# Heads of the last unit but one turned behind their own block, short cycles moved from tile 65 to tile 75, last projection pair stored behind its cycle's block

## The chip, the core and the metric

The kernel runs on one core of a Trainium2 chip. A core has five engines that run side by side, each in its own order: TensorE (PE, matmuls; PEld is its weight load), VectorE (DVE), ScalarE (ACT), GpSimd (POOL) and SyncE (SP, which issues the transfers between the core's memory and the chip's main memory). The metric is the device time of one execution in microseconds (us), as the median of several runs.

## The reference

A layer norm of x (2048 tokens of 512 numbers), then two branches on it, joined by a gate:

```python
xn = _layernorm(x, axis=-1)
# s: attention with 32 heads of 16, softmax over all 2048 keys
q, k, v = (xn @ wqkv) split into 3 x 32 heads x 16
p = softmax(q k^T * 16**-0.5)
s = (p v) @ wo
# g: gated unit with 1792 inner columns, no nonlinearity inside, silu at its end
g = silu(((xn @ w_gate) * (xn @ w_up)) @ w_down)
return x + s * g
```

All inputs and outputs are float32.

## The kernel before

**Units, tiles, cycles.** Attention is cut into 32 units: unit i is a group of 4 heads (8 groups) with 512 queries (4 column chunks). A unit has 16 key tiles of 128 keys, so tiles count from 0 to 511, and tile n belongs to unit n // 16. For each tile and head TensorE computes the transposed scores ("t", L755), ACT their exps into a tile e (L757), and TensorE multiplies the exps by the values ("pv", L774; "last" for unit 31). Ahead of that, by 86 matmuls, run the untransposed scores ("s", L733), of which DVE takes the maxima (L735); a unit's maxima go through main memory into two extra rows of the queries.

The work is put out in cycles of BLOCK = 5 tiles. SHORT gives some cycles another length. A cycle holds 20 t, 20 s (none after the scores have run out, near tile 491) and a filler pair; then `values` puts out, in this order: the list `before_values`, the maxima of a finished unit, one step of `heads`, the block (the pv matmuls of the cycle's tiles, and the sum), the list `behind_values`, and up to four bulk transfers. The last cycle has two tiles and ends with the block of unit 31's last tiles.

**The block** (`part_block`) multiplies into one bank per unit, and then adds it: the first block of a unit is copied by ACT (L782), later ones are copied by ACT to the one tile `part` (L787) and added by POOL (L788, shown at L100, the helper that records POOL's and SP's instructions), and from tile 492 on DVE adds straight from the bank (L784). When a unit's tile 15 is in, `finish(i)` turns and scales its heads: transpose (L799), reciprocal (L803), product (L805), transpose back (L810) and a store to OD (L811); then unit i is in `finished`. `finish` is a generator: for units before 28 it yields once, for units 28 and 29 twice, for unit 30 never. It is put on a list and stepped later: `heads` one step per cycle ahead of the block, `last_group` (units 28 and 29) at three places within a cycle's items.

**The filler** is a generator of pairs of matmul groups, one for the lower 64 rows of the array and one for the upper 64; `Filler.item` puts out one matmul of a half, and fetches the next pair as soon as one is used up. If the generator yields nothing, there is no pair until the start of the next cycle, and that cycle has no filler if there is none then either. LIMIT caps the items per half that a cycle takes. In order the filler gives:

- 13 projection pairs of keys and queries (`proj_pair`). At a pair's end ACT copies one half to `qr`, DVE the other (`rest`, on `before_values`), and `store` (on `behind_values`) lets POOL split both into a high and a low part in `hl`, of which there is one buffer, and stores each to KD or QD.
- 80 pairs of the gated unit (`ffn`): g and u pairs (product on DVE, L449; ACT's copy of g, L494) and y pairs. Its pool is opened where the projection's pool is closed, and takes over its memory.
- the output projection (`ending`): z pairs for chunk 3 (all but its last rows), then z0, z1 and z2, two of four token tiles each (`two_tiles(c, t)`), each of which waits in `until(c)` for the split rows of chunk c. `prepare` reloads the rows of a chunk from OD when its units are in `finished` (the last fourth of chunk 2 needs unit 30), and POOL splits them (`o_split`) six steps later; `end` multiplies a tile by its gate (L581), and the sum with x (L590) and the store follow behind the block.

Each cycle's items are ordered by a written list in ORDERS where there is one for its counts, and evenly otherwise. DVE, ACT, POOL and TensorE keep the order of the program; the issues of SP are ordered by the scheduler. In the last stage there are five banks for the transposed scores. The end of the program (`last_heads`, L815 on, and four pairs of matmuls at L683) turns the heads of unit 31 and finishes the last four token tiles.

Of the kernel before, what the change touches and what calls it, by code (L numbers as in the profile page):

```python
# [22 lines left out]
NC = S // 512  # L23
# [43 lines left out]
}  # L67
SHORT = {65: 3, 68: 3}
LIMIT = {65: 12, 491: 12}
BULK = 4  # L70
EBUFS = 20
HBUFS = 1
# [13 lines left out]
def body(ctx, tc, x, wqkv, wo, wg, wu, wd, out):  # L86
# [23 lines left out]
    def dma(dst, src):  # L110
        sync.dma_start(dst, src)
# [42 lines left out]
    def psum(tag, name):  # L154
        ps, bufs = fst["ps"]
        return ps.tile([P, 512], F32, tag=tag, name=name, bufs=bufs[tag])
# [11 lines left out]
    def flush():  # L168
        while waiting:
            waiting.pop(0)[1]()  # L170
# [6 lines left out]
    before_values, behind_values, lighter = [], [], [False]  # L177

    def run_all(queue):
        while queue:  # L180
            queue.pop(0)()
# [6 lines left out]
    def part_tile():  # L188

        return ep.tile([P, 512], F32, name="part", bufs=1)  # L190
# [84 lines left out]
    def late():  # L275
        return now[0] > NU * NT - LEAD // 4
# [82 lines left out]
    def qk_weights(m, which):  # L359
        c0 = which * D + m * P  # L360
        return split(f"w{which}", wqkv[:, c0:c0 + P])
# [21 lines left out]
    def proj_pair(m, which):  # L383

        two = Pair([("misc", f"p{w}_{m}_{c}") for _, w, c in which],
                   [terms(lambda d: ws[0][:, d], lambda d: ws[1][:, d],
                          lambda d: xh[c][:, d], lambda d: xl[c][:, d], ND) for ws, _, c in which])
        yield two
        outs = two.outs
        raws = [qp.tile([P, D], F32, name="qr", bufs=QBUFS) for _ in outs]  # L390
        fst["high"] = nc.scalar.activation(raws[0], outs[0], AF.Copy)

        def rest():
            nc.vector.tensor_copy(raws[1], outs[1])
            behind_values.append(lambda: store(raws))

        def store(raws):
            for o, (_, w, c) in zip(raws, which):
                hl = qp.tile([P, 2, D], F32R, name="hl", bufs=HBUFS)
                split_rows(o, hl[:, 0], hl[:, 1])  # L400
                qk_store(hl, m, w, c)
        before_values.append(rest)
# [59 lines left out]
    def gu_weights(f):  # L462
        fs = slice(f * P, (f + 1) * P)
        return [split(n, w[:, fs]) for n, w in (("w1", wg), ("w0", wu))]
# [223 lines left out]
    NU = NG * NC  # L688
# [71 lines left out]
    def block(todo):  # L760

        for i in sorted({i for i, _, _ in todo}):
            part_block(i, [t for t in todo if t[0] == i])

    def part_block(i, todo):

        g = i // NC
        whole = i == NU - 1
        o = fst["last"] if whole else psum("b", f"pv{i}")
        for n, (_, kt, es) in enumerate(todo):  # L770
            halves = [slice(0, 256), slice(256, 512)] if whole and kt == NT - 1 else [slice(0, 512)]
            for c, j in ((c, j) for c in halves for j in range(4)):
                h0 = (4 * g + j) * VW
                nc.tensor.matmul(o[32 * j:32 * j + 32, c], V[:, kt, h0:h0 + 32], es[j][:, c],  # L774
                                 start=(kt if whole else n) == 0, stop=kt == NT - 1 if whole else n == len(todo) - 1,
                                 skip_group_check=whole)
        if whole:
            if todo[-1][1] == NT - 1:
                last_heads(o)
        elif todo[0][1] == 0:  # L780
            sums[i] = keep.tile([P, 512], F32, name="acc", bufs=2)
            nc.scalar.activation(sums[i], o, AF.Copy)  # L782
        elif late():
            nc.vector.tensor_tensor(sums[i], o, sums[i], op=OP.add)  # L784
        else:
            part = part_tile()
            nc.scalar.activation(part, o, AF.Copy)  # L787
            pool.tensor_tensor(sums[i], sums[i], part, op=OP.add)  # L788
        if not whole and todo[-1][1] == NT - 1:
            (last_group if NU - NC <= i < NU - 2 else heads).append(finish(i))  # L790

    def finish(i):

        g, c = divmod(i, NC)
        tr = keep.tile([P, 16, 32], F32, name="tr", bufs=1)
        acc = sums.pop(i)
        late = i >= NU - NC
        flat = "p b e -> p (b e)"
        nc.vector.transpose(tr.rearrange(flat), acc)  # L799
        rc = keep.tile([P, 16, 1], F32, name="rc", bufs=1)  # L800
        if NU - NC <= i < NU - 2:
            yield
        nc.vector.reciprocal(rc, tr[:, :, DH:DH + 1])  # L803
        over = rc.to_broadcast([P, 16, DH])
        (nc.vector if i >= NU - NC else pool).tensor_tensor(tr[:, :, 0:DH], tr[:, :, 0:DH], over, op=OP.mult)  # L805
        if not late:
            yield
        elif i < NU - 2:
            yield
        nc.vector.transpose(acc, tr.rearrange(flat))  # L810
        dma(OD[c][4 * g:4 * g + 4], acc)  # L811
        finished.add(i)


    def last_heads(o):  # L815

        tr = keep.tile([P, 16, 32], F32, name="tr", bufs=1)
        rc = keep.tile([P, 16, 1], F32, name="rc", bufs=1)
        both, fst["t"] = [fst["fp"].tile([P, 512], F32, name="g", bufs=2).bitcast(F32R) for _ in range(2)]
        back = keep.tile([P, 512], F32, name="acc", bufs=2)  # L820
        both = both.rearrange("p (b e) -> p b e", e=32)
        flat = "p b e -> p (b e)"
        for h in range(2):
            c, b = slice(256 * h, 256 * h + 256), slice(8 * h, 8 * h + 8)
            nc.vector.transpose(tr[:, b].rearrange(flat), o[:, c])
            nc.vector.reciprocal(rc[:, b], tr[:, b, DH:DH + 1])
            nc.vector.tensor_tensor(tr[:, b, 0:DH], tr[:, b, 0:DH], rc[:, b].to_broadcast([P, 8, DH]), op=OP.mult)
            pool.tensor_copy(both[:, b, 0:DH], tr[:, b, 0:DH])
            pool.tensor_tensor(both[:, b, DH:32], tr[:, b, 0:DH], both[:, b, 0:DH], op=OP.subtract)
        for h in range(2):  # L830
            c, b = slice(256 * h, 256 * h + 256), slice(8 * h, 8 * h + 8)
            nc.vector.transpose(back[:, c], both[:, b].rearrange(flat).bitcast(F32))
            nc.scalar.activation(fst["t"][:, c], back[:, c], AF.Copy)


    def run(gen):
        for _ in gen:
            pass
# [124 lines left out]
    def filler(wq0):  # L963
        yield from proj_pair(0, [(wq0, 0, 2), (wq0, 0, 3)])
        for m in range(1, NG // 2):
            wk, wq = fst["qk", m]
            for c in range(NC):
                if c == 2 and m + 1 < NG // 2:
                    fst["qk", m + 1] = qk_weights(m + 1, 1), qk_weights(m + 1, 0)
                yield from proj_pair(m, [(wk, 1, c), (wq, 0, c)])  # L970
                if m == 1 and c:
                    bulk.extend(lambda n=n, src=src[c], c=c, d=d: dma(XD[c][n][:, d].bitcast(F32), src[:, d].bitcast(F32))
                                for n, src in enumerate((xh, xl)) for d in range(ND))
                if m == NG // 2 - 1 and c == NC - 2:
                    nxt = gu_weights(0)
        run_all(before_values)
        run_all(behind_values)
        run_all(bulk)
        flush()
        qkv.close()  # L980
        fst["fp"] = ffp.enter_context(tc.tile_pool(name="ffn", bufs=1, reuse_waits="tile"))
        yield from ffn(nxt)
# [3 lines left out]
    heads, last_group = [], []  # L986
# [92 lines left out]
    with tc.manual_schedule(engines=ORDERED):  # L1079
        with banks_of(EARLY_BUFS):  # L1080
            fil = Filler(filler(early()))
        place_of = banks_of(BUFS)
        q, m, n = 0, LEAD, 0
        while n < NU * NT:
            tiles = min(SHORT.get(n, BLOCK), NU * NT - 2 - n) or 2
            ends = n + tiles == NU * NT
# [4 lines left out]
            if fil.done:  # L1091
                fil = Filler(ending())
            f = fil.begin(LIMIT.get(n, 99))
            last = min(4 * (n + tiles), TOTAL - 4 * (not ends))
# [51 lines left out]
```

## Time and profile before

| | us |
|---|---|
| median of 3 runs (lowest, highest) | 1686.39 (1685.56, 1687.9) |
| the profiled execution, its time | 1685.45 |
| its span, first to last instruction | 1683.7 |
| PE busy | 1667.0 (99%) |
| DVE busy | 1418.4 (84%) |
| ACT busy | 1188.1 (71%) |
| POOL busy | 736.6 (44%) |

The mean granted clock of TensorE is 0.995 of full speed. Matmuls are pipelined, so a busy PE in the table is not PE at its peak. In the profile's rows a group of instructions is "line engine operation out<-in xcount"; in a timeline the start and the length stand ahead of it, and idle time of the engine before it, with what ended it, in brackets behind it. In a table of stretches each row has the bounds, the length, the busy time of the five engines with counts, the granted clock, the DMA engines' share and GB/s.

### The profile page before, as it was taken

How to read it: one execution, taken by the hardware profiler on the slowest of the kernel's cores; microseconds unless marked ns; L12 is line 12 of the kernel's file. 1: busy time of each engine (PE TensorE's matmuls, PEld its weight loads, DVE VectorE, ACT ScalarE, POOL GpSimd, SP SyncE). 2: the span in 40 equal slices, each digit the busy share in tenths (PEclk: the TensorE clock that was granted, in tenths of full speed). 3: DMA queues.
4: the chain of work that ended last, by engine and by line, in shares of the span. 5: the costliest groups of instructions: out<-in, count | busy, mean ns of one | idle time of the engine just before them, and what ended most of it. 6: DMA issues, size and time to landing. Idle time of an engine off the chain costs nothing.

```text
span 1683.7 us, 35313 instructions
## 1 busy us (share of the span) xinstructions
PE 1667.0 (99%) x13702; PEld 1123.8 (67%) x13702; DVE 1418.4 (84%) x2477; ACT 1188.1 (71%) x2553; POOL 736.6 (44%) x772
## 2 busy tenths in 40 slices
PE   9999999999999999999999999999999999999997
PEld 6776666666666676666667666766676676666654
DVE  7888888888888998798889888888988898899822
ACT  6367777776766787677677767867787677678673
POOL 5214434651634456155252733624365262455551
PEclk9999999999999999999999999999999999999998
DMA  7434335321321313121142212302233121133241
GB/s 272 139 123 173 134 120 160 104 66 36 86 55 55 105 53 96 43 74 55 37 103 91 72 50 64 101 18 64 80 99 91 36 74 36 46 104 98 71 129 51
DMA packets 124467, 145.94 MB, mean 87 GB/s; under 512 B 13644, under 2 KB 75340, under 8 KB 123532
## 3 DMA queue, kind: packets, MB, share of 16 engines
q1 hardware_dynamic: 124300, 143.69, 27.7%
q8 instruction: 108, 1.77, 0.4%
q14 instruction: 59, 0.48, 0.1%
HBM read 95.94 MB, written 47.45 MB: 85 GB/s over the span
## 4 chain that ended last, share of the span: by engine, by line
PE 96%; DVE 2%; ACT 0%; DMA 0%; POOL 0%; issue 0%; SPq 0%; DVEq 0%; POOLq 0%; ACTq 0%
PE pv L774 26%; PE s L733 16%; PE t L755 14%; PE g L355 10%; PE u L355 9%; PE y L355 9%; PE p L355 4%; PE z L355 2%; DVE mx L735 2%; PE last L774 1%; PE v L307 1%; PE v L327 1%; PE p L307 1%; PE warm L865 0%; DMA KD<-hl 0%; PE xT L283 0%
## 5 line engine op out<-in xcount | busy, mean ns | idle before, releaser
L735 DVE TENSOR_REDUCE mx<-s 128x1 f32<-128x512 f32 x2048 | 1244.9, 682 | 192.7 <-PE t L755 134.3
L757 ACT ACTIVATE e<-t 128x512 f32<-128x512 f32 x2048 | 1024.4, 669 | 23.9 <-PE t L755 20.3
L755 PE MATMUL t<-qs,ks 50*128 50x512 f32 x2048 | 789.9, 406 | 1.9 <-DVE mx L735 1.4
L733 PE MATMUL s<-ks,qs 48*128 48x512 f32 x2048 | 757.4, 407 | 1.5 <-ACT part L787 1.4
L733 PEld LDWEIGHTS s<-ks,qs 48*128 48x128 f32 x2048 | 367.7, 186 | 140.3 <-issue 83.1
L774 PE MATMUL pv<-e,V 128*32 128x512 f32 x3968 | 446.5, 595 | 0.0
L755 PEld LDWEIGHTS t<-qs,ks 50*128 50x128 f32 x2048 | 375.0, 186 | 67.7 <-ACT e L757 20.3
L100 POOL TENSOR_TENSOR acc<-acc,part 128x512 f32<-128x512 f32 x93 | 121.0, 1301 | 445.6 <-ACT part L787 445.5
L774 PEld LDWEIGHTS pv<-e,V 128*32 128x32 f32 x3968 | 118.8, 110 | 264.9 <-issue 256.9
L787 ACT ACTIVATE part<-pv 128x512 f32<-128x512 f32 x93 | 55.6, 598 | 323.1 <-PE pv L774 318.4
L355 PE MATMUL g<-fh,w1h 64*128 64x512 f32 x448 | 181.6, 405 | 0.0
L355 PE MATMUL u<-fh,w0h 64*128 64x512 f32 x448 | 177.6, 397 | 0.0
L355 PE MATMUL g<-fh,w1l 64*128 64x512 f32 x448 | 177.2, 396 | 0.0
L355 PE MATMUL u<-fl,w0h 64*128 64x512 f32 x448 | 176.9, 395 | 0.0
L355 PE MATMUL g<-fl,w1h 64*128 64x512 f32 x448 | 176.5, 394 | 0.0
L355 PE MATMUL u<-fh,w0l 64*128 64x512 f32 x448 | 175.5, 392 | 0.0
L355 PE MATMUL y<-dh,hl 64*128 64x512 f32 x448 | 147.0, 393 | 0.0
L355 PE MATMUL y<-dh,hh 64*128 64x512 f32 x448 | 145.5, 396 | 0.0
L355 PE MATMUL y<-dl,hh 64*128 64x512 f32 x448 | 143.6, 394 | 0.0
L100 POOL TENSOR_TENSOR tr<-tr,rc 128x256 f32<-128x256 f32 x28 | 17.4, 621 | 227.8 <-DVE rc L803 227.8
L355 PEld LDWEIGHTS g<-fh,w1l 64*128 64x128 f32 x448 | 83.7, 187 | 5.5
L355 PEld LDWEIGHTS g<-fh,w1h 64*128 64x128 f32 x448 | 83.4, 186 | 4.6
(228 smaller groups left out, 2334.7 us busy)
## 6 DMA issues: line engine op xcount, KB each, us to landing
w1r<-in_wg_dram SPq DMA_DIRECT2D x56, 256.0 KB
w0r<-in_wu_dram SPq DMA_DIRECT2D x56, 256.0 KB
wdr<-in_wd_dram SPq DMA_DIRECT2D x56, 256.0 KB
ks<-KD SPq DMA_DIRECT2D x64, 192.0 KB
qs<-QD SPq DMA_DIRECT2D x64, 192.0 KB
KD<-hl SPq DMA_DIRECT2D x16, 512.0 KB
OD<-acc SPq DMA_DIRECT2D x31, 256.0 KB
QD<-hl SPq DMA_DIRECT2D x14, 512.0 KB
```

The source lines that it names most:

```text
L100: got = getattr(self.engine, name)(*args, **kw)
L307: nc.tensor.matmul(o[:, part], l(d), r(d)[:, part], start=k == d == 0 and not begun, stop=k == 2 and d == ND - 1, skip_group_check=begun)
L327: nc.tensor.matmul(outs[k], l[LOWER], r[LOWER], start=k == 0 and n == 0, stop=(stop or k == 0) and n == len(low) - 1, skip_group_check=k == 1)
L355: nc.tensor.matmul(self.outs[k], l[rows], r[rows], start=opens and not half, stop=closes, skip_group_check=half == 1)
L733: nc.tensor.matmul(o, QS[i][b:b + KB, pr, t * P:(t + 1) * P], k[b:b + KB, pr, kc * 512:(kc + 1) * 512], start=True, stop=True)
L735: nc.vector.tensor_reduce(MX[i][:, j, t, kc:kc + 1], o, axis=AX.X, op=OP.max)
L755: nc.tensor.matmul(o, k[b:b + KR, pr, kt * P:(kt + 1) * P], QS[i][b:b + KR, pr], start=True, stop=True)
L757: nc.scalar.activation(e, o, AF.Exp, scale=DH ** -0.5)
L774: nc.tensor.matmul(o[32 * j:32 * j + 32, c], V[:, kt, h0:h0 + 32], es[j][:, c], start=(kt if whole else n) == 0, stop=kt == NT - 1 if whol ...
L787: nc.scalar.activation(part, o, AF.Copy)
```

## The change

Three things are changed.

- SHORT and LIMIT: the two cycles of three tiles, which began at tiles 65 and 68, now begin at 75 and 78; the limit of 12 items per half on the pair that is spread over both moves along. From tile 81 on the cycles have the bounds that they had.
- Behind the last projection pair the filler no longer empties `before_values` and `behind_values` itself, at the end of cycle 60's items; it yields nothing instead, and the gated unit's pool is opened at the start of the next cycle.
- `finish(30)` is run to its end as soon as its block is put out, in the cycle of tile 491, instead of being put on `heads`, which the next cycle (tile 496) steps ahead of its block. Units 28 and 29 stay on `last_group`, the others on `heads`.

```diff
-SHORT = {65: 3, 68: 3}
-LIMIT = {65: 12, 491: 12}
+SHORT = {75: 3, 78: 3}
+LIMIT = {75: 12, 491: 12}
...
         if not whole and todo[-1][1] == NT - 1:
-            (last_group if NU - NC <= i < NU - 2 else heads).append(finish(i))
+            if i == NU - 2:
+                run(finish(i))
+            else:
+                (last_group if i >= NU - NC else heads).append(finish(i))
...
                 if m == NG // 2 - 1 and c == NC - 2:
                     nxt = gu_weights(0)
-        run_all(before_values)
-        run_all(behind_values)
+        yield
         run_all(bulk)
         flush()
         qkv.close()
```

## The prediction

> **What bounds the kernel now.** I read the page first, then the chain of waits, then busy time by stretches cut at the block boundaries, then each engine's timeline at the two places that the diff touches.
>
> ```profile
> span 1683.7 us, 35313 instructions
> PE 1667.0 (99%) x13702; PEld 1123.8 (67%) x13702; DVE 1418.4 (84%) x2477; ACT 1188.1 (71%) x2553; POOL 736.6 (44%) x772
> PE 96%; DVE 2%; ACT 0%; DMA 0%; POOL 0%; issue 0%; SPq 0%; DVEq 0%; POOLq 0%; ACTq 0%
> ```
>
> TensorE carries 96% of the chain that ends last, so time is won only where TensorE waits, runs at a lower granted clock, or is fed at another engine's pace. The stretches show two such places, both beside the edits. First the cycles of tiles 60, 65, 68, 71 and 76, one row each, with their sum (columns: us, busy time of each engine, granted clock, DMA share, GB/s):
>
> ```profile
> 275.42:290.47 15.05, 15.05 (x130) 10.46 (x130) 12.71 (x21) 11.64 (x25) 10.30 (x11) 1.00 0.41 148
> 290.47:299.29 8.82, 8.82 (x73) 5.38 (x74) 7.27 (x12) 6.50 (x15) 1.00 (x3) 1.00 0.80 201
> 299.29:312.15 12.86, 10.97 (x78) 6.69 (x74) 9.53 (x16) 7.29 (x14) 9.80 (x10) 0.87 0.43 144
> 312.15:327.21 15.06, 15.06 (x131) 10.27 (x130) 13.55 (x26) 11.04 (x24) 8.71 (x9) 1.00 0.29 89
> 327.21:342.30 15.09, 15.09 (x131) 10.41 (x130) 12.75 (x21) 11.63 (x25) 8.76 (x10) 1.00 0.29 81
> sum 66.88, PE 64.99 PEld 43.22 DVE 55.81 ACT 48.09 POOL 38.58; mean PE 13.00 PEld 8.64 DVE 11.16 ACT 9.62 POOL 7.72
> ```
>
> Two cycles of three tiles hold the same work, yet one takes 8.82 us and the next 12.86, with 1.89 us of TensorE idle and a clock of 0.87. The timelines of POOL, ACT and DVE name the cause:
>
> ```profile
> 288.78 0.61 POOL L100 CAST hl<-qr 128x512 fp32r<-128x512 f32 x1
> 298.51 0.61 POOL L100 CAST hl<-qr 128x512 fp32r<-128x512 f32 x1 [7.74 <-DMA KD<-hl]
> 300.45 1.27 POOL L100 TENSOR_TENSOR acc<-acc,part 128x512 f32<-128x512 f32 x1
> 301.75 0.60 ACT L787 ACTIVATE part<-pv 128x512 f32<-128x512 f32 x1 [4.74 <-POOL acc L100]
> 301.75 0.71 DVE L799 STREAM_TRANSPOSE tr<-acc 128x512 f32<-128x512 f32 x1 [3.57 <-POOL acc L100]
> ```
>
> POOL runs the splits of the last projection pair ahead of the sum (L788) of tile 60's block. The second split waits 7.74 us for the single hl buffer to be stored; the sum queued behind it ends at 301.7, and on it hang ACT's copy of the next block (the one part buffer) and DVE's turning of unit 3's heads. Both engines stop, then TensorE.
>
> The second place is the end: items and block of tile 496's cycle, of 501's, of 506's, and of the last two tiles:
>
> ```profile
> 1621.40:1629.88 8.48, 8.48 (x49) 5.69 (x45) 3.22 (x6) 7.94 (x17) 0.00 (x0) 1.00 0.57 179
> 1629.88:1634.31 4.43, 4.43 (x43) 1.20 (x42) 1.95 (x4) 1.97 (x5) 0.00 (x0) 1.00 0.61 202
> 1634.31:1643.13 8.82, 8.54 (x25) 4.14 (x21) 0.00 (x0) 8.23 (x18) 1.88 (x2) 0.73 0.48 137
> 1643.13:1650.27 7.14, 7.14 (x42) 1.62 (x42) 0.00 (x0) 1.68 (x4) 0.00 (x0) 0.61 0.00 0
> 1650.27:1658.10 7.83, 7.83 (x68) 6.78 (x65) 0.16 (x1) 7.19 (x17) 0.00 (x0) 1.00 0.01 2
> 1658.10:1661.67 3.57, 3.57 (x33) 0.94 (x32) 2.33 (x4) 0.87 (x2) 0.00 (x0) 1.00 0.28 104
> 1661.67:1669.14 7.47, 7.18 (x60) 5.89 (x56) 0.00 (x0) 4.31 (x10) 0.00 (x0) 1.00 0.06 23
> 1669.14:1671.10 1.96, 1.93 (x25) 0.68 (x24) 1.29 (x2) 0.27 (x1) 0.00 (x0) 1.00 0.00 0
> ```
>
> Cycle 501 (third and fourth row) has no filler, only about 20 transposed scores at the pace of ACT's exps. The clock falls, and the same block that took 4.43 us takes 7.14. The filler pairs that might have lain there sit in cycle 506 and in the last, which has exps for eight tiles' heads only.
>
> **The change, part by part.**
>
> *Projection pair.* No instruction goes. The generator now hands back nothing after the last projection pair, so its DVE copy and its POOL splits are put out by the ordinary end of cycle 60: copy before the block, splits behind the block's sums. POOL's order turns from split, split, sum into sum, split, split. ACT's copies of this block and a regular cycle's end, with the waits for hl elsewhere, give the new times:
>
> ```profile
> 289.66 0.60 ACT L787 ACTIVATE part<-pv 128x512 f32<-128x512 f32 x1 [2.92 <-PE pv L774]
> 268.54 0.61 POOL L100 CAST hl<-qr 128x512 fp32r<-128x512 f32 x1 [4.15 <-DMA KD<-hl]
> 283.01 0.61 POOL L100 CAST hl<-qr 128x512 fp32r<-128x512 f32 x1 [3.58 <-DMA KD<-hl]
> 299.20 1.30 POOL L100 TENSOR_TENSOR hl<-qr,hl 128x512 fp32r<-128x512 f32 x1
> 322.85 0.60 ACT L494 ACTIVATE g<-g 128x512 f32<-128x512 f32 x1
> 324.68 0.68 DVE L449 TENSOR_TENSOR g<-u,g 128x512 f32<-128x512 f32 x1
> 327.37 0.60 ACT L787 ACTIVATE part<-pv 128x512 f32<-128x512 f32 x1 [3.92 <-PE pv L774]
> ```
>
> The sum runs at about 290.3 to 291.6, ten us sooner; ACT and DVE no longer wait for it. The first split (2.0 us, 298.51 to 300.50 above) follows until 293.6, the wait for hl (3.6 to 4.2 us in the two rows above) until 297.5, the second split until 299.5, and its store lands, by the same waits, near 303.4. What is queued behind it on POOL is the weight split for the next pair, wanted only at 305.5, and the next sum, wanted at 320.5. So the moved splits cost nothing there. SP's store queue moves by the same 2 to 3 us; the pair's keys and queries are for units far later.
>
> What is late next is the gated-unit stage. Its pool takes the memory of the projection pool, and its g tile may lie on hl or qr. Before, that g was first written at the end of the second short cycle. Now the first gated pair ends with cycle 65, which starts at 290.47: a regular cycle (312.15 above) has its g copy 10.7 us after the start and the product 12.5, so g is written at 301.2, and behind it DVE's product (0.68), the transpose of unit 3's heads (0.71) and a reciprocal have to fit before the next reduces, shortly after the block ends at 305.5. That leaves slack until about 303.8. The 303.4 for the store lies just inside. Bounds: no cost; or, with the 7.74 us wait on both stores, a landing near 311 less queueing, 3.5 us of stall and 2 us of lower clock behind it. I take no cost, because two of the three waits shown are short, and the loads that crowd the long one (DMA share 0.80 from 290.47) now have two us more to go through before the store is issued.
>
> *Short cycles.* Tiles 65 to 81 become 5, 5, 3, 3 instead of 3, 3, 5, 5, with the limit of 12 on the pair at 75; from 81 on the program is as before, with the same count of pairs and blocks. An undisturbed short cycle is 8.82 us. So the five cycles take 15.05 + 15.06 + 15.09 + 2 x 8.82 = 62.84, against 66.88: **4.0 us saved**.
>
> *Heads of unit 30.* Their four DVE steps and one store move from cycle 496's end to right behind tile 495's sum. The rows, DVE then SP then POOL:
>
> ```profile
> 1621.68 0.69 DVE L784 TENSOR_TENSOR acc<-pv,acc 128x512 f32<-128x512 f32 x1 [14.68 <-PE pv L774]
> 1628.49 0.70 DVE L799 STREAM_TRANSPOSE tr<-acc 128x512 f32<-128x512 f32 x1
> 1630.71 0.32 SPq L100 DMA_DIRECT2D OD<-acc  x1
> 1632.78 0.69 SPq L100 DMA_DIRECT2D wdr<-OD  x1
> 1638.75 0.61 POOL L100 CAST hl<-wdr 128x512 fp32r<-128x512 f32 x1 [18.72 <-DMA wdr<-OD]
> 1634.90 9.90 ACT L757 ACTIVATE e<-t 128x512 f32<-128x512 f32 x20 [3.05 <-PE t L755]
> ```
>
> The sum ends at 1622.4; DVE is idle behind it, so the four steps (2.2 us from 1628.49 to the store) cost nothing there, and the store goes out at 1624.7. The reload and POOL's split (2.0 us from 1638.75) end 10.0 us after the store's issue now, so by then at 1634.7. Since `finished` holds unit 30 one cycle sooner, prepare() puts out the reload in cycle 496, and the pair z2_0/z2_1 is begun with cycle 501 at 1634.3. The late fourth rows of its operands come in as items 10 to 12 of 24, about 2.8 us in: 2.4 us of slack. SP issues the two transfers between a residual load and the outputs of the pair before, which nothing near waits for.
>
> Cycle 501 then has 48 filler items. Each half of the array takes 34 turns instead of cycle 506's 32 in 7.83 us, so 8.3 us; ACT's pace, 9.90/20 = 0.495 us per exp, lets the twentieth score go when the fifteenth exp frees its bank, at 0.6 + 7.4 us. I take 8.6 (ends 8.0 and 9.4). With TensorE fed as in cycle 496 the clock stays at 1.00 and the block takes 4.43. Cycle 506 takes the other pair, 7.83 + 3.57 as now. The last two tiles have no filler: eight exps, 0.59 + 8 x 0.495 = 4.55 us, and some ten matmuls of the block behind the last exp at 1.96/24 us, together 5.4 instead of 9.43. From 1634.31 to 1671.10 are 36.79 us; after 8.6 + 4.43 + 7.83 + 3.57 + 5.4 = 29.83: **7.0 us saved**.
>
> *Behind the last block.* The chain has, and the granted clock at the earlier place shows:
>
> ```profile
> 1674.57 1.18 DVE ks L590 x2
> 1675.74 1.81 DVE y L581 x3
> 1636.00:1638.00 2.00, 2.00 (x6) 0.73 (x5) 0.00 (x0) 2.00 (x5) 0.00 (x0) 1.00 0.99 226
> 1640.00:1642.00 2.00, 2.00 (x6) 1.18 (x5) 0.00 (x0) 2.00 (x5) 0.71 (x1) 0.50 0.00 0
> ```
>
> The two additions of the pair z2_2/z2_3 now run in cycle 506 and leave the chain: 1.18 us at most, nothing at least. The last cycle is now thinly fed, as 501 was, where the clock was 0.50 some 4 to 6 us in; the last eight matmuls would then come slower and take back about half. I take **0.5 us**. The Trainium skill, "TensorE: Matmul & The Clock Gate", Part 1, puts the same thing as a rule: half clock after an idle window of about 3.4 us, full clock after a busy one. The trace agrees: full clock lasted 3.7 to 5.7 us into cycle 501, and the level behind it is 0.50.
>
> **Sum.** 4.0 + 7.0 + 0.5 = 11.5 us. The profiled execution took 1685.45 us (span 1683.7), 0.94 below the median of 1686.39; 1685.45 - 11.5 = 1673.95, and against the median 1674.9. I say 1675.0.
>
> **Rivals.**
>
> *The clock falls inside the last cycle.* For it: cycle 501's rows. Against: here the thin stretch is 4.6 us, not 8.8, behind a full-clock block. The remaining block matmuls run at the 0.18 us of 7.14/40 instead of 0.08: one us more, 1676.0. The rule named above says so only if its window falls inside the stretch.
>
> *The g tile waits.* For it: the common memory and the slack of only 0.6 us. Against: the store is issued with a calmer DMA. The head's gain shrinks from 4.0 to between 2 and -1.5: 1677 to 1680.5.
>
> *The pair is not there for cycle 501.* If the filler is not handed the pair there, or waits in the cycle for its rows as long as it gains, only the head's gain remains: 1682.4. If the stores are not reordered either, nothing changes: 1686.4. Against both: the program's order decides the one, and POOL keeps that order in the other.
>
> *Slower.* One mechanism: TensorE, in order, meets z2_0's fourth rows before they are split and stands, with the scores and exps behind it. The stall costs its length and some 3 us at half clock; it eats the whole gain at 8.5 us and is 0.2% slower at 12, for which the chain from store to split would have to last 10.0 + 2.4 + 12 = 24 us. It lasts 10.0 here, beside a DMA share of 0.48 to 0.61.
>
> **Chances.** Forecast 0.47, clock in the last cycle 0.18, g tile 0.17, only the head's gain or about it 0.09, no change 0.05, slower 0.04. A change of 0.2% (3.4 us) is about what can be told from none; below 1683.0 lie the first three and two thirds of the fourth: faster 0.88, same 0.08, slower 0.04. The range of 1672.5 to 1681.0 takes the g tile's bound, cycle 501 at 8.0 to 9.4, the full 1.18 us and the 1.5 us by which the runs shown differ from their median; it leaves out the last three cases.
>
> **What the next profile would show.** Right: POOL's sum of tile 60's block ahead of both hl casts; no idle of ACT on that sum; clock 1.00 from 290 to 342; two short cycles of about 8.8 us at tiles 75 and 78; unit 30's store near six us sooner against its block; z matmuls among the exps of cycle 501 and a block of 4.4 us behind it; none in the last two tiles. Wrong: ACT's g copy waiting on a DMA near 301, z waiting on POOL in cycle 501, or a cycle 501 without z.

## The result, and the profile after

The changed kernel takes 1676.69 us in the median of four runs (1674.98 to 1678.92), the kernel before 1686.51 in four: a ratio of 0.9942, with a 95% interval of 0.9925 to 0.9959. The forecast was 1675.0, between 1672.5 and 1681.0. The profiled execution is the slowest of the four, 1678.92 us with a span of 1677.0, which is 6.7 less than the span before.

Three places make up these 6.7 us. First the cycles of tiles 60, 65, 70, 75 and 78, in busy time by stretches (columns as before), and from the timelines of POOL and ACT the sum of tile 60's block, the second split and the first copy of g:

```profile
275.32:290.37 15.05, 15.05 (x130) 10.20 (x130) 12.70 (x21) 11.64 (x25) 8.86 (x10) 1.00 0.41 149
290.37:305.36 14.99, 14.99 (x130) 10.16 (x130) 12.46 (x21) 11.04 (x24) 8.60 (x9) 1.00 0.63 184
305.36:320.87 15.51, 15.51 (x130) 9.75 (x130) 14.95 (x29) 11.33 (x24) 11.12 (x12) 1.00 0.35 109
320.87:329.85 8.98, 8.98 (x74) 5.60 (x74) 7.28 (x12) 6.50 (x15) 6.83 (x7) 1.00 0.30 94
329.85:338.70 8.85, 8.85 (x74) 5.59 (x72) 7.87 (x13) 7.56 (x15) 3.17 (x3) 1.00 0.37 103
```

```profile
290.24 1.30 POOL L100 TENSOR_TENSOR acc<-acc,part 128x512 f32<-128x512 f32 x1 [1.25 <-ACT part L787]
299.51 0.61 POOL L100 CAST hl<-qr 128x512 fp32r<-128x512 f32 x1 [6.04 <-DMA KD<-hl]
304.37 0.60 ACT L494 ACTIVATE g<-g 128x512 f32<-128x512 f32 x1 [3.51 <-DMA QD<-hl]
```

The stall is gone: 63.38 us instead of 66.88, the clock 1.00 throughout, TensorE never idle. The sum runs at 290.24, ahead of both splits. The new wait is there as well: ACT's copy of g stands 3.51 us for the store of the projection pair's queries, and the cycle of tile 70 takes 15.51 instead of 15.06. Saved: 3.5 us.

Second, the cycles of tiles 491 and 496 (items, block, items, block), then 501, 506, the last two tiles, and what lies behind:

```profile
1604.40:1613.39 8.99, 8.97 (x49) 5.80 (x45) 0.00 (x0) 8.77 (x21) 8.75 (x8) 0.92 0.16 54
1613.39:1620.50 7.11, 7.11 (x42) 1.64 (x41) 0.00 (x0) 1.67 (x4) 3.14 (x3) 0.62 0.45 137
1620.50:1628.94 8.44, 8.44 (x48) 5.67 (x44) 5.28 (x9) 7.93 (x17) 0.00 (x0) 1.00 0.47 147
1628.94:1635.10 6.16, 6.16 (x43) 1.56 (x42) 0.00 (x0) 1.98 (x5) 1.88 (x2) 0.72 0.79 260
1635.10:1643.76 8.66, 8.66 (x72) 7.04 (x69) 1.01 (x2) 8.04 (x19) 0.00 (x0) 1.00 0.00 0
1643.76:1648.20 4.44, 4.44 (x43) 1.21 (x42) 1.48 (x3) 1.97 (x5) 0.00 (x0) 1.00 0.34 122
1648.20:1655.99 7.79, 7.79 (x68) 6.98 (x64) 0.24 (x1) 7.22 (x17) 0.00 (x0) 1.00 0.00 0
1655.99:1659.56 3.57, 3.57 (x33) 0.94 (x32) 2.25 (x4) 0.84 (x2) 0.00 (x0) 1.00 0.21 77
1659.56:1662.14 2.58, 2.36 (x12) 1.03 (x8) 0.00 (x0) 2.05 (x5) 0.00 (x0) 1.00 0.27 103
1662.14:1665.20 3.06, 3.06 (x25) 1.07 (x24) 0.00 (x0) 1.98 (x5) 0.00 (x0) 1.00 0.00 0
1665.20:1677.00 11.80, 2.23 (x9) 1.35 (x8) 7.00 (x15) 0.83 (x2) 4.46 (x6) 0.85 0.25 89
```

Cycle 501 now has the pair z2_0/z2_1 (72 matmuls instead of 25 in the items), its clock is 1.00 and its block takes 4.44 us instead of 7.14. The pair could start there because the store of unit 30's heads was issued at 1623.72 and POOL had split the reloaded rows by 1632.1, ahead of the cycle's start at 1635.10:

```profile
1623.72 0.32 SPq L100 DMA_DIRECT2D OD<-acc  x1
1630.84 1.27 POOL L100 TENSOR_TENSOR dh<-wdr,hl 128x512 fp32r<-128x512 f32 x1
```

The last two tiles take 5.64 us instead of 9.43. From cycle 501 to the end of the last block are 30.10 us instead of 36.79: 6.7 saved; behind it 11.8 instead of 12.6: 0.8 saved.

Third, a loss: the blocks of tiles 491 and 496 took 7.11 and 6.16 us here, at clocks of 0.62 and 0.72, where the profile before has 4.42 and 4.43 at 1.00. That is 4.4 us, and neither cycle's matmuls were changed. 3.5 + 6.7 + 0.8 - 4.4 = 6.6 of the 6.7. Whether this loss belongs to the change was the main question for the experiments.

### The profile page after: what moved, and what is told of

It reads as the page before. It is cut to its first block, busy times and chain, and to the rows that moved or that the text cites. A ratio compares the mean times of both kernels' runs of the same rounds, so it can differ in the third digit from the quotient of the medians.

```text
span 1677.0 us, 35313 instructions
## 1 busy us (share of the span) xinstructions
PE 1662.9 (99%) x13702; PEld 1121.3 (67%) x13702; DVE 1418.6 (85%) x2477; ACT 1187.8 (71%) x2553; POOL 736.5 (44%) x772
## 4 chain that ended last, share of the span: by engine, by line
PE 97%; DVE 2%; ACT 0%; issue 0%; POOL 0%; DMA 0%; DVEq 0%; ACTq 0%
PE pv L774 26%; PE s L733 16%; PE t L755 14%; PE g L355 10%; PE u L355 9%; PE y L355 9%; PE p L355 4%; PE z L355 2%; DVE mx L735 1%; PE last L774 1%; PE v L327 1%; PE v L307 1%; PE p L307 1%; PE xT L283 0%; PE v L331 0%
```

## The experiments

The kernel before was timed again beside them; its medians were 1686.46 (35 runs), 1686.87 (23), 1686.94 (17) and 1687.32 (11), its single runs lying between 1681.2 and 1691.5. Ratios are against the runs in the same group.

**The parts apart.** The first two runs undo one part each.

```diff
# e1: of the change, only
+            if i == NU - 2:
+                run(finish(i))
...
# e2: the rest of it, without these lines
```

> Only the heads of unit 30 turned behind their own block; the short cycles and the projection pair's store stay as before. My theory: the parts are independent, and this one gives what the profiles show from cycle 501 on: 36.79 us become 30.1 up to the last block's end (6.7), and 12.6 become 11.8 behind it (0.8), so 7.5 less than before, about 1679.0, with z matmuls in cycle 501 and a block of 4.4 us behind it. In the profile of the changed kernel the clock fell in the cycles of tiles 491 and 496 instead and cost 4.4; if that is chance from run to run, single runs lie between 1679 and 1683.5. Rival: those falls belong to the other two parts (they shift where the end of the kernel lies in time); then the clock is 1.00 in both cycles here in every run, and the time 1679.0 with a small spread. The head of the kernel keeps its stall: the two short cycles take 8.8 and 12.9 us.

> The store behind its block and the short cycles at 75 and 78, without the part on unit 30's heads. My theory: 3.5 us less than before, about 1683.0: from cycle 60's start to tile 81 it takes 63.4 us instead of 66.9, and ACT's first copy of g waits some 3.5 us for the store of the projection pair's queries, which costs about 0.45 in the cycle of tile 70. The end is as before: no z in cycle 501, a block of about 7.1 us behind it. Rival: the parts overlap in what they save and together give less than their sum; then this one gives 2 or less, above 1684.5.

Measured: e1 1681.78 us (0.9969, 0.9956 to 0.9982), e2 1682.24 (0.9978, 0.9964 to 0.9991). That is 4.7 and 4.2 us less by the medians, together 8.9, and the whole change gave 9.8 with an interval of 6.9 to 12.6. The parts add up within what can be measured. But e1 missed its expected 1679.0 by 2.8 us. In its profile the end is as expected (30.11 us from cycle 501 to the end of the last block, 11.8 behind it); the 7.5 us, however, were read against a single profile of the kernel before, in which the block of cycle 501 takes 7.14 us. In e2, e3 and e4, whose end is that of the kernel before, it takes 5.80, 5.54 and 6.89. The single runs of e1 go from 1676.36, at a mean clock of 0.999, to 1686.12 at 0.994, wider than I expected. The blocks of its profile, one row for each of the last five cycles (in the timeline of TensorE, where a block of forty matmuls at full clock shows as 4.50; start, length):

```profile
1617.21 6.20 PE L774 MATMUL pv<-e,V 128*32 128x512 f32 x40
1632.09 5.80 PE L774 MATMUL last<-e,V 128*32 128x512 f32 x40
1646.52 4.50 PE L774 MATMUL last<-e,V 128*32 128x512 f32 x40
1658.75 3.64 PE L774 MATMUL last<-e,V 128*32 128x512 f32 x32
1664.91 3.07 PE L774 MATMUL last<-e,V 128*32 128x512 f32 x24
```

The clock fell in 491 and 496 here too, without the other two parts, so the rival that they cause it is ruled out. In e2's profile it did not fall there.

**The halves of the head's change.**

```diff
# e3: only this
-        run_all(before_values)
-        run_all(behind_values)
+        yield
# e4: only this
-SHORT = {65: 3, 68: 3}
-LIMIT = {65: 12, 491: 12}
+SHORT = {75: 3, 78: 3}
+LIMIT = {75: 12, 491: 12}
```

> Only the order: the projection pair's store behind the sum of its block, with the short cycles left at 65 and 68. My theory: the order alone takes POOL's sum out from behind the wait for hl, and g is first written at the end of the second short cycle, after the store has landed, so nothing waits: the five cycles take 62.8 us, 4.0 less than before, about 1682.5, no worse than with the short cycles moved. Rival: in a short cycle POOL has not the time for both splits, the weight splits and the sums, and the next sum comes late instead (needed 8.8 us on, where a full cycle gives 15): ACT waits on POOL again for 1 to 3 us, and the time is 1684 to 1686.5.

> Only the short cycles moved to 75 and 78; the projection pair's splits stay ahead of the sum on POOL. My theory: the sum still waits behind the split until about 301.7, but with a full cycle at tile 65 ACT's next copy of a block comes at 305.5 and DVE's turning of unit 3's heads about 302, so the late sum is in time; g waits for the store as in the changed kernel. 3 to 4 us less than before, about 1683.0: either half of the head's change is enough by itself. Rival: the order on POOL is what counts, and without it the stall only moves; then it is within 1 us of before, about 1686.

Measured: e3 1683.70 us (0.9982, 0.9971 to 0.9993), e4 1682.00 (0.9978, 0.9967 to 0.9990). The runs alone can't tell these from e2, and e3's median lies between the times of its theory (1682.5) and of its rival (1684 to 1686.5), but the traces decide. From the start of tile 60's block to the start of tile 81's cycle there are 56.35 us before, 52.85 with the change, 52.6 in e2, 52.45 in e3 and 52.46 in e4. ACT's copies and POOL's sum, first two rows e3, last three e4:

```profile
299.34 0.60 ACT L787 ACTIVATE part<-pv 128x512 f32<-128x512 f32 x1 [2.47 <-PE pv L774]
308.29 0.60 ACT L787 ACTIVATE part<-pv 128x512 f32<-128x512 f32 x1 [1.98 <-PE pv L774]
```

```profile
300.06 1.29 POOL L100 TENSOR_TENSOR acc<-acc,part 128x512 f32<-128x512 f32 x1
302.96 0.60 ACT L494 ACTIVATE g<-g 128x512 f32<-128x512 f32 x1 [2.21 <-DMA QD<-hl]
305.40 0.60 ACT L787 ACTIVATE part<-pv 128x512 f32<-128x512 f32 x1 [1.84 <-PE pv L774]
```

Both theories of mine hold: in no copy is POOL the releaser. In e3 the sum is early. In e4 it is nearly as late as before (it starts at 300.06, before at 300.45), but with a full cycle at tile 65 it is wanted at 305.4 and no longer at 299.3. Either half by itself takes out the stall; the second adds nothing, and e3 is even free of the wait for g, which is first written at the end of its second short cycle. In e4 the wait for g is there, but it ends at 302.96 and the stretch is no longer for it.

**The wait for g.**

```diff
             if c == 0:
+                begin = [fp.tile([P, D], F32, name="wdr", bufs=2),
+                         fp.tile([P, 512], F32, name="g", bufs=2)]
             y = fp.tile([P, 4, D], F32, name="y")
# and the first wdr and g are taken from begin
```

> The changed kernel with the first tiles g and wdr of the gated unit's pool taken ahead of its others, so that they lie where the projection pool's activations lay and not on hl or qr. My theory: ACT's first g copy then waits for no store (3.5 us in the changed kernel's profile), and the cycle of tile 70 takes 15.06 us instead of 15.51: 0.45 less, too little for the runs to tell, so it is read in the profile. Rival: the wait is not one for memory but the order of the transfers, and ACT waits as before, or the wait moves to dl on POOL, whose memory now lies on hl, and POOL's next sum comes late.

Measured: 1676.41 us (0.9934, 0.9917 to 0.9950; six runs). ACT's first copy of g in its trace stands behind nothing:

```profile
300.73 0.60 ACT L496 ACTIVATE g<-g 128x512 f32<-128x512 f32 x1
305.24 0.60 ACT L789 ACTIVATE part<-pv 128x512 f32<-128x512 f32 x1 [3.92 <-PE pv L776]
```

The stretch from tile 60's block to tile 81 is 52.45 us, 0.4 less than with the change. So it was the shared memory, and the price of the wait is 0.4 us in the profiles; the runs can't tell e6 from the changed kernel.

**The falls of the clock.** If thin feeding of TensorE brings them about, more work in cycles 491 and 496 must stop them.

```diff
                 fil.item(h) if kind == "F" else place(h) if kind == "t" else scored(h)
+                if n in (491, 496) and k >= len(order) - 20 and k % 2:
+                    nc.tensor.matmul(fst["last"], fst["w"][0][:, 0, 0:P],
+                                     fst["w"][1][:, 0], start=True, stop=True)
```

> The changed kernel with ten more matmuls of 128x512 among the last items of each of the cycles of tiles 491 and 496, into the bank of unit 31, which is first written for good behind them; their results are overwritten. My theory: the clock falls in these two cycles because TensorE is thinly fed there, and whether it falls is chance from run to run; the added matmuls take time that TensorE has while it waits for ACT's exps. Then the clock is 1.00 in both cycles in the profile, both blocks take 4.4 us (7.1 and 6.2 in the profile of the changed kernel), every run shows a mean clock of 0.998 or more, and the median is about 1674.5 with less than 2 us between the runs. Rival one: the added matmuls lie on the path and cost their 20 x 0.22 = 4.4 us: 1677 to 1681. Rival two: the falls have nothing to do with how TensorE is fed; then they go on, and the runs spread over 4 us as they do now.

> The changed kernel with both: the added matmuls in the cycles of tiles 491 and 496, and g and wdr taken first. If both theories hold: 1674.0, all runs within 2 us, 12.4 less than before.

Measured: e5 1684.13 us (0.9983, 0.9974 to 0.9993), e8 1685.09 (0.9986, 0.9977 to 0.9995). Items and block of e5's cycle 491, and the end of these items on TensorE:

```profile
1603.61:1616.87 13.26, 13.26 (x58) 7.06 (x55) 0.00 (x0) 9.81 (x22) 11.54 (x10) 1.00 0.13 42
1616.87:1621.30 4.43, 4.43 (x42) 1.20 (x41) 0.00 (x0) 0.87 (x2) 0.00 (x0) 1.00 0.97 305
```

```profile
1615.14 0.50 PE L755 MATMUL t<-qs,ks 50*128 50x512 f32 x2
1615.57 0.51 PE L1105 MATMUL last<-fl,fh 128*128 128x512 f32 x1
1616.01 0.50 PE L755 MATMUL t<-qs,ks 50*128 50x512 f32 x2
1616.44 0.50 PE L1105 MATMUL last<-fl,fh 128*128 128x512 f32 x1
```

The clock held in both profiles, but the first rival held as well, at twice its price: the items take 13.26 us instead of 8.8. The twelve runs of e5 also spread over 4.2 us, at mean clocks of 0.995 to 0.999, where less than 2 us and at least 0.998 were expected; those of e8 spread over 1.5. Each change between 128 rows and 50 costs a step of 0.43 us, where z matmuls of 64 rows come every 0.23. That points to the kind of matmul as the cost, and a second try has 64 rows:

```diff
-                    ... fst["w"][0][:, 0, 0:P], fst["w"][1][:, 0], ...
+                    ... fst["w"][0][LOWER, 0, 0:P], fst["w"][1][LOWER, 0], ...
```

> As the run with added matmuls in the cycles of tiles 491 and 496, but these are of 64 rows (the lower half of the array), like the fillers. That run held the clock at 1.00 and lost 4.5 us in each of the two cycles, with steps of 0.43 us wherever a matmul of 128 rows stood beside one of 64 or 50. My theory: it is that change of rows that cost, since weights are then not loaded ahead; with 64 rows the steps are 0.23 us, the items take 8.5 to 9.5 us, and the clock stays: about 1674.5 to 1675.5. Rival: any added work lies on the path here: 1678 or more.

Measured: 1675.33 us (0.9932, 0.9918 to 0.9946), all six runs between 1674.51 and 1675.81. Its cycles 491 and 496:

```profile
1604.52:1613.30 8.78, 8.76 (x58) 6.22 (x54) 0.00 (x0) 8.53 (x20) 8.49 (x8) 1.00 0.11 39
1613.30:1617.73 4.43, 4.43 (x42) 1.19 (x40) 0.00 (x0) 1.91 (x4) 3.07 (x3) 1.00 0.18 46
1617.73:1626.20 8.47, 8.47 (x58) 6.25 (x54) 5.20 (x9) 7.94 (x17) 0.00 (x0) 1.00 0.67 211
1626.20:1630.70 4.50, 4.50 (x44) 1.27 (x42) 0.08 (x1) 1.97 (x5) 1.30 (x2) 1.00 0.86 277
```

Ten useless matmuls more in each cycle cost nothing, and the clock holds in this profile. The weights show the difference to e5: there a 128-row matmul's weights are loaded at its own start (both at 1615.57), here a 64-row matmul's are loaded 0.24 us ahead of it (at 1609.28 for the matmul at 1609.52).

The profiles together say more than this one alone. Of the nine kernels whose cycles 491 and 496 are fed as before, seven have at least one block slowed there, to between 5.5 and 7.2 us (after, e1, e3, e4, e6, and below e9 and e12), and two have none (before and e2). Of the five in which these cycles have added matmuls (e5, e8, e11 and e13), or the evenly spread ones of e10 below, none has. So the loss seen in the profile after is not the change's: it occurs with and without each part, and thin feeding is its likely cause. The profile before was a lucky draw in these two cycles. By time the gain isn't shown: e11's median lies 1.1 us below that of e6, and the intervals of the two overlap.

The same with the work that is there, spread by leaving out the written order for these counts:

```diff
-    (20, 0, 12, 12): (
+    (20, 0, 12, 13): (
```

> The changed kernel without the written order for 20 t and 12 fillers per half, so that the cycles of tiles 491 and 496 spread their fillers evenly instead of ending on seven t alone. My theory: the clock falls in the thinly fed stretch at the end of these cycles; spread out, no stretch is that thin, both blocks take 4.4 us, and the runs lie near 1674.5 with a mean clock of 0.998 or more. Rival: what counts is the share of the whole cycle that TensorE works, which does not change; then the clock falls as often or more often, and the median stays at 1676 to 1678.

Measured: 1676.44 us (0.9939, 0.9923 to 0.9955), six runs from 1675.35 to 1676.97, mean clocks of 0.997 to 0.999. In the profile both blocks take 4.43 and the items 8.9 each instead of 8.8 and 8.5. The median is the rival's (1676 to 1678) and not the expected 1674.5, so by time the rival stands. The profile speaks against it, though one profile can't show that the clock never falls. The evenly spread items take 0.6 us more, which eats part of what a held clock gains.

**What cycle 501 gains by.** Two runs give the kernel before more work in cycle 501 and leave its filler where it was.

```diff
# e9: behind each of its last sixteen t
+                if n == 501 and k >= 4:
+                    nc.tensor.matmul(psum("misc", "warm"), fst["w"][0][:, 0, 0:P], ...)
# e12: instead, behind each t, one matmul of 64 rows in each half
+                    for d, rows in enumerate((LOWER, UPPER)):
+                        nc.tensor.matmul(spare[d], fst["w"][0][rows, 0, 0:P], ...)
```

> The kernel before with sixteen more matmuls of 128x512 among the twenty scores of cycle 501, into the two free banks, and nothing else; their results are read by no one. It parts the two gains of the filler pair in cycle 501. My theory: what that cycle gains is the clock alone: with TensorE fed the block behind it takes 4.4 us instead of 7.1, the items stay near 8.8 at ACT's pace, and the time falls by 2.7 in a run where the clock would have fallen wholly, some 2 us in the median, 1684 to 1685; the other 4 us of the change come from the last two tiles having no filler, which stay here at 9.4. Rival: the clock falls there for another reason, the block stays at 7.1, and the added work costs up to 3 us: 1686 to 1689.

> The kernel before with a matmul of 64 rows in each half behind each of the twenty scores of cycle 501, in place of the matmuls of 128 rows that made that cycle 19 us long and did not hold the clock. My theory: at 30 turns of 0.23 us per half the items stay near ACT's pace, 8.8 us, the clock stays at 1.00, and the block behind takes 4.4 us: about 2 to 2.7 us less than before, 1684 to 1684.5 against a median of 1686.5. The rest of the change's gain at the end, some 4 us, is the last two tiles without filler. Rival: the clock falls there although TensorE is fed; the block stays at 7.1 us and the time is 1686.5 or more.

Measured: e9 1697.29 us (1.0065, 1.0048 to 1.0082). It does not part the two gains: 128 rows between 50 made the cycle 19 us long, and the clock fell in spite of it. e12: 1685.59 (0.9992, 0.9980 to 1.0005), not to be told from before by its time, and between what the theory (1684 to 1684.5) and the rival (1686.5 or more) had for it. Its cycle 501, items and block:

```profile
1637.60:1646.41 8.81, 8.81 (x65) 5.88 (x61) 0.00 (x0) 8.18 (x18) 1.90 (x2) 1.00 0.27 77
1646.41:1650.84 4.43, 4.43 (x43) 1.20 (x42) 0.00 (x0) 1.73 (x4) 0.00 (x0) 1.00 0.01 4
```

The items take 8.81 us and the block 4.43: fed with forty useless matmuls the cycle is within 0.2 us of its length with the filler pair. So in the profiles what the pair gains in 501 is the clock: 2.7 us where it would have fallen as in the profile before, 1.1 where as in e3. The runs make two groups, five from 1681.1 to 1684.5 at clocks of 0.997 to 0.998 and seven from 1685.5 to 1688.3 at 0.993 to 0.995; in the profiled one, of the second group, cycles 491 and 496 had fallen. The rest of the change's gain up to the last block's end, 9.43 - 5.64 = 3.8 us, is the last two tiles without filler; in e12, where they keep it, they take 9.44.

**A version beyond the change.** It takes the 64-row matmuls, g and wdr first, and six matmuls where TensorE stands idle behind the last block:

```diff
+        spare = psum("misc", "warm")
+        for _ in range(6):
+            nc.tensor.matmul(spare, fst["w"][0][:, 0, 0:P], fst["w"][1][:, 0], start=True, stop=True)
         banks = []
         for t in range(4):
             banks.append(psum("b", f"z{NC - 1}_{t}"))
```

> The changed kernel with the 64-row matmuls in the cycles of tiles 491 and 496, with g and wdr taken first, and with six matmuls of 128 rows between the last block and the last eight, where TensorE stands idle for 2.95 us (results read by no one). In the profile of the run with 64-row matmuls the clock fell behind the last block: the last eight matmuls came every 0.43 us instead of 0.23, and 13.1 us lay behind the block instead of 11.8. My theory: 0.45 us less for g, and up to 1.3 less at the end if six matmuls (1.4 us) are enough to hold the clock: 1674 to 1675, the lowest median so far. Rival: six are too few or the clock has fallen before them; then they take 0.43 us each, 2.6 us in the 2.95 of idle time, and nothing is gained at the end: 1675.

Measured: 1675.07 us (0.9927, 0.9915 to 0.9939), all six runs between 1674.69 and 1675.44. First the last matmuls of the 64-row run, then of this one:

```profile
1663.72 0.79 PE L683 MATMUL z<-hl,g 128*128 128x512 f32 x1 [2.95 <-ACT g L836]
1664.31 0.63 PE L683 MATMUL z<-dh,g 128*128 128x512 f32 x1
```

```profile
1660.68 1.66 PE L683 MATMUL warm<-fl,fh 128*128 128x512 f32 x6
1663.70 0.50 PE L688 MATMUL z<-hl,g 128*128 128x512 f32 x1 [1.36 <-ACT g L841]
1664.04 0.40 PE L688 MATMUL z<-dh,g 128*128 128x512 f32 x1
```

The last eight matmuls come every 0.23 us again, so the clock was held, and the last DVE instruction ends 8.1 us behind the last block instead of 9.4: the 1.3 us foreseen. But the whole stretch behind the block is 12.8 us against 13.1 in the 64-row run, because 4.7 us lie behind that DVE instruction instead of 3.7. The trace has a transfer of instructions there (one packet on the instruction queue); of all runs only e6, e8 and e13 have it and the longer end, the three that take g and wdr first. That it costs the missing 1 us is likely and not shown; it would be more than the 0.4 us that taking g first saves.

The median of 1675.07 can't part the theory (1674 to 1675) from the rival (1675). It is the lowest median and the narrowest set of runs, 1.6 us under the changed kernel; both were timed in different groups and the intervals overlap, so a gain over the changed kernel is likely and not shown.

## Why the prediction was right, point by point

- **The place of the stall and its cause**: right. POOL's sum behind the wait for hl, ACT and DVE behind the sum. Taken as 4.0 us, measured 3.5.
- **The g tile**: wrong in its mechanism, and cheap. The estimate that the store would land at 303.4, inside the slack to 303.8, was the mis-sized term: the first wait for hl was 6.04 us where I took 3.9, g waited until 304.37, and that cost 0.4 us (e6). ACT's copy of g waiting on a DMA is a sign of being wrong that the prediction names. Its rival on g, at 2 us or more, had the right mechanism and too large a price. The slack itself fits e4, where g waits until 302.96 at no cost.
- **Which edit does it.** I had the reordering take out the stall and the short cycles only move. e4 shows that the move alone does it too. The sum was right, since only one of the two is paid.
- **Cycle 501**: 8.6 + 4.43 foreseen, 8.66 + 4.44 measured; 506 as foreseen. The last two tiles 5.4 foreseen, 5.64 measured. Together 7.0 foreseen, 6.7 measured. The rows were split 3.0 us before cycle 501's start, where 0.4 us behind it was foreseen.
- **Behind the last block**: 0.5 foreseen, 0.8 measured in the profile after, where the last eight matmuls came every 0.23 us. In the 64-row run they came every 0.43 and 13.1 us lay behind the block, against 12.6 before: that takes back the whole gain and more, not the half that I assumed.
- **What was missing**: that the clock may fall in cycles 491 and 496. I read them as 1.00 out of one profile and put the fall only into the last cycle, as a rival of 1 us. (Its price set 0.18 us per matmul against 0.08, the pace of the last 24; forty matmuls of a full-clock block take 4.43/40 = 0.11 each, which makes it 0.7.) In the profile after the fall cost 4.4 us. What it does to the medians is not shown, since e9 and e12, which are the kernel before up to cycle 501, have it too.
- **Luck in the total.** The parts measured in the profiles are 3.5 + 6.7 + 0.8 = 11.0 us of the 11.5 foreseen, the medians differ by 9.8. Part of the 11.0 is a draw: the profile before had its clock fall furthest in cycle 501 and not at all in 491 and 496. The distance of 1.7 us between forecast and median lies within the interval of the change, 6.9 to 12.6 us, and how it divides among such draws stays open.
- **The rule on the clock.** The Trainium skill, "TensorE: Matmul & The Clock Gate", Part 1, has the gate judge windows of about 3.4 us that run free of the kernel. That would let the same cycles fall in some executions and not in others; the mean clocks of the changed kernel's four runs, 0.996 to 0.999, fit it, but no kernel was profiled twice, and no run here measured the window itself. The prediction says that the trace agrees with a fall behind an idle window. It agrees in the time until the fall and in the level of 0.50, but TensorE is busy for 8.54 of the 8.82 us of those items in the profile, so the trace shows no idle window of 3.4 us.

## What to carry to other kernels

Ask of a stall behind one small buffer what is queued behind the waiting instruction, and when that is next wanted: here either taking the sum out of the queue or lengthening the cycle ahead of the next use was enough, and the two did not add. Filler work is worth most where TensorE would otherwise wait for another engine: in cycle 501 it took no time, it spared the last two tiles 3.8 us, and it held the clock, whose fall is paid in the dense block behind. A clock read in one profile, fallen or at 1.00, is one draw: look at the spread of the runs and their mean clocks before counting on it.

## What the runs showed of the hardware

- Between a matmul of 128 rows and one of 50 the step is 0.43 us at a clock of 1.00, both ways, where matmuls of 64 and 50 rows in the two halves of the array come every 0.23 us per half and those of 128 rows among themselves every 0.23.
- A TensorE that the profile shows busy without a gap does not keep the clock up by that alone. In the run with 128-row matmuls between the scores of cycle 501 (e9), busy time and clock by stretches:

```profile
1638.00:1642.00 4.00, 4.00 (x10) 1.67 (x10) 0.00 (x0) 3.54 (x7) 1.80 (x2) 1.00 0.01 3
1642.00:1646.00 4.00, 4.00 (x7) 1.61 (x6) 0.00 (x0) 1.79 (x3) 0.00 (x0) 0.55 0.00 0
1646.00:1650.00 4.00, 4.00 (x7) 1.61 (x6) 0.00 (x0) 1.79 (x3) 0.00 (x0) 0.50 0.00 0
```
